# Scores of two chunks in one PSUM bank, fourteen transposes a pair, and the weight steps of DVE ahead of the divisions

## The chip, the cores and the metric

The kernel runs on one core of one Trainium2 chip. The metric is the device time of one execution in microseconds (us). Five engines work side by side, each through its own list of instructions in the order in which they were written: TensorE (PE, with its weight loads as PEld), VectorE (DVE), ScalarE (ACT), GpSimd (POOL) and SyncE (SP), which here only issues loads and stores. They wait for one another by semaphores.

## The reference

Attention, then a network with squared ReLU, then a gated network, all in float32:

```python
scores = scale * np.matmul(q, k.transpose(0, 1, 3, 2))      # 2 batches, 12 heads, 448 x 64
attn = np.exp(causal(scores) - max); attn = attn / (attn.sum(-1) + 1e-9)
x = np.matmul(attn, v)                                      # -> 896 tokens x 768
h = x @ w_in; x = (s * np.maximum(h, 0.0) ** 2 + b) @ w_out           # 768 -> 2048 -> 768
x = (1 / (1 + np.exp(-(x @ w_gate))) * (x @ w_val)) @ w_out2          # 768 -> 1536 -> 768
```

## The kernel before

The twelve pairs of heads are worked one after the other; the two heads of a pair lie side by side on the 128 partitions. The 448 queries of a head are cut into 7 chunks of 64, and chunk c needs the first (c + 1) x 64 keys, so that its scores are 64 to 448 columns wide. The two networks that follow are products of split numbers: an operand is held as a high and a low part, and three matmuls make one product.

For a pair, the work goes through these functions. `scores` (matmul at L242) writes the scores of one chunk into a PSUM bank of its own. `chunk` runs `softmax`: DVE adds the mask and takes the maximum (L229, two instructions, one of them the read of the maximum), ACT takes the exponential and the row sum (L232). `divide` (L261) has DVE make the reciprocals r of the sums (L265, L266) and POOL scale the seven chunks (L271). `turned` (L281) transposes the probabilities in blocks of 128 x 128 on PE (L291), four to a bank, four banks a pair; DVE copies the first and third bank (L279), ACT the second and fourth (L276). The fourth bank holds the blocks on the diagonal, of which only 64 rows are wanted. `values` (L313) multiplies with v into a bank of its own, `output_hi` (ACT, L276) and `output_lo` (DVE, L326) split the result into x_hi and x_lo.

The loop over i from 3 to 11 (L418 to L440) staggers this: pass i makes the scores of pair i, the values of pair i - 3, the softmax of pair i, the reciprocals and divisions of pair i - 1, and the transposes of pair i - 2. Its text is the order of each engine (`tc.manual_schedule()`): on PE a pass is scores, values, transposes; on DVE seven maxima with r behind the second, one step of the weights' splitting, copy, x_lo, copy; on ACT seven exponentials with x_hi behind the fifth, then two copies. The chunks go in the order

```python
ORDER = (0, 1, 6, 4, 3, 5, 2)
```

PSUM has eight banks: seven of tag "w", which scores and transposes take in turn, and one for the values. A bank is taken again only when its readers are through.

Into passes 4 to 10 the splitting of the first network's weights is woven, one step a pass (`split_steps`, L68; `step`, L354). A step of ACT (Abs at L75, the high part at L96) stands at the end of the pass, in passes 4, 8 and 10. A step of DVE stands behind the seventh maximum: L77 and L80 in pass 5, L85 in pass 6, L89 in pass 7, L98 in pass 9. L77 needs the Abs of pass 4, L98 the high part of pass 8.

Before the loop a prologue works pairs 0 to 2. The first pair's q and k come in four loads, two issued by SP and two by ACT; its chunks are made in the order 0 to 6. Behind the loop come the rest of the attention, between it the first matmuls of the first network (`fill`, L334), and the values of pair 11 end the attention.

Of the kernel before, what the change touches and what calls it, by code (L numbers as in the profile page):

```python
# [13 lines left out]
ALU = mybir.AluOpType  # L14
# [8 lines left out]
def body(ctx: ExitStack, tc: tile.TileContext, qk, vp, w_in, w_out, s, b, w_gate, w_val, w_out2, outT):  # L23
# [145 lines left out]
    with tc.tile_pool(name="at", bufs=2) as at:  # L169
# [5 lines left out]
        KF, KS = D, D + S + 4 * D  # L175
        Q_AT = {0: 0, 5: KF + S, 6: KF + S + D, 2: KS - 2 * D, 1: KS - D, 3: KS + 5 * D, 4: KS + 6 * D}
        ORDER = (0, 1, 6, 4, 3, 5, 2)

        PO, n = {}, 0
        for c in (0, 1, 2, 3, 4, 6, 5):  # L180
            PO[c], n = n, n + (c + 1) * D
        ALL = n

        mask = at.tile([P, S], F32, name="mask", bufs=1)
        nc.gpsimd.memset(mask, 0.0)
        for j in range(2):
            rows = slice(j * D, (j + 1) * D)
            nc.gpsimd.affine_select(
                out=mask[rows, S - D:], in_=mask[rows, S - D:], compare_op=ALU.is_ge, fill=NEG,
# [5 lines left out]
        HALF = slice(0, (NK - 1) * (NC + 2) + 1, NC + 2)  # L195
        for t in ptTs:
            nc.gpsimd.memset(t[D:, HALF], 0.0)
# [4 lines left out]
        def load_qk(i, engine=nc.sync):  # L202
# [31 lines left out]
        def scores(i, c):  # L234

            t = st[i]
            sc = t["sc", c] = bank("sc", "w")
            q0, n, k0 = Q_AT[c], (c + 1) * D, KF if c in FRONT else KS
            for j in range(2):
# [3 lines left out]
                    sc[j * D:(j + 1) * D, :n], t["qk"][rows, q0:q0 + D], t["qk"][rows, k0:k0 + n],  # L243
# [37 lines left out]
        def turned(i, copies=(dve, act, dve, act)):  # L281
# [21 lines left out]
            put(copies[3], t["ptT"][:D, HALF], [(2 * k, k) for k in range(NK)], D)  # L303
# [60 lines left out]
        with tc.manual_schedule():  # L364
# [53 lines left out]
            for i in range(3, N):  # L418
# [156 lines left out]
```

## Time and profile before

| | |
|---|---|
| median of three runs | 577.74 us (577.49 to 577.78) |
| the profiled execution | 577.84 us, its span 576.1 us |
| granted clock of TensorE in it | 1.00 |
| attention loop, passes 3 to 11 | 15.56 to 66.40 us of the span |
| end of the last attention product | 77.49 us |

The span is the time between the first and the last instruction that the profiler shows, the execution's own time has a little around it. Times in the timeline count from the start of the span. A matmul's end in it is modelled, and a line of the timeline may join several instructions of a line of the kernel (x28); the start of the next line then tells better how long the first took than its own duration. A line of the chain of waits says on which engine the work ran that the end of the kernel hung on.

### The profile page before, as it was taken

Reading aid. Unit: us, or ns where it says so; the run is one execution under the profiler, and the core shown is the slowest. Engines: PE = TensorE matmul, PEld = TensorE weight load, DVE = VectorE, ACT = ScalarE, POOL = GpSimd, SP = SyncE. Lnnn points to the kernel's source line nnn. Section 1 sums busy time; section 2 is a strip of 40 time slices with the busy share of each in tenths; the row PEclk is TensorE's granted clock in tenths of the full one; section 3 lists DMA queues with packets and bytes.
Section 4 is the critical chain, followed back from the end, with each engine's and each line's share of the span. In section 5 each row is a group of like instructions: output and inputs, shape, how many; then the busy total and the mean of one; then the engine's idle time right before and its main releaser. Section 6 shows DMA issues by size and latency. Waiting matters only on the chain.

```text
span 576.1 us, 8214 instructions
## 1 busy us (share of the span) xinstructions
PE 570.3 (99%) x3176; PEld 507.6 (88%) x3177; DVE 386.2 (67%) x705; ACT 266.8 (46%) x514; POOL 42.4 (7%) x93
## 2 busy tenths in 40 slices
PE   8999999999999999999999999999999999999997
PEld 4666789899999999999999999999999999999996
DVE  5899676999999766565647766666666666654000
ACT  6989846667776522223215333333333333332100
POOL 3676600000000000000000000000000000000000
PEclk9999999999999999999999999999999999999999
DMA  7745013345444333333322333333333333540000
GB/s 247 303 153 188 19 56 110 109 166 160 134 141 142 118 111 101 104 117 135 110 110 81 115 105 106 103 104 108 110 109 109 106 109 110 196 143 32 33 32 34
DMA packets 16168, 67.39 MB, mean 117 GB/s; under 512 B 2048, under 2 KB 3968, under 8 KB 16128
## 3 DMA queue, kind: packets, MB, share of 16 engines
q1 hardware_dynamic: 15696, 65.94, 34.7%
q10 hardware_dynamic: 432, 0.92, 0.5%
q8 instruction: 25, 0.41, 0.3%
q14 instruction: 15, 0.12, 0.1%
HBM read 64.10 MB, written 2.75 MB: 116 GB/s over the span
## 4 chain that ended last, share of the span: by engine, by line
PE 92%; ACT 4%; DVE 3%; issue 0%; DVEq 0%; ACTq 0%
PE acc L120 81%; PE po L313 4%; PE tp L291 3%; PE sc L242 3%; ACT pt L232 2%; DVE g L164 1%; DVE wt L85 0%; DVE wt L89 0%; ACT whi L96 0%; PE cold L373 0%; ACT ga_hi L165 0%; DVE wt L77 0%; DVE ga_lo L166 0%; DVE wlo L98 0%; ACT g L162 0%
## 5 line engine op out<-in xcount | busy, mean ns | idle before, releaser
L120 PE MATMUL acc<-x_hi,whi 128*128 128x448 f32 x480 | 175.6, 366 | 0.0
L120 PE MATMUL acc<-x_hi,wlo 128*128 128x448 f32 x480 | 175.4, 365 | 0.1
L120 PE MATMUL acc<-x_lo,whi 128*128 128x448 f32 x480 | 175.3, 365 | 0.0
L98 DVE TENSOR_TENSOR wlo<-wt,whi 128x768 fp32r<-128x768 f32 (+1 forms) x70 | 65.7, 939 | 74.5 <-ACT whi L96 74.3
L96 ACT ACTIVATE whi<-wt 128x768 fp32r<-128x768 f32 (+1 forms) x70 | 57.9, 827 | 122.2 <-PE acc L120 116.2
L120 PEld LDWEIGHTS acc<-x_hi,wlo 128*128 128x128 f32 x480 | 90.2, 188 | 7.6 <-DVE wlo L98 0.5
L120 PEld LDWEIGHTS acc<-x_hi,whi 128*128 128x128 f32 x480 | 90.2, 188 | 7.4 <-ACT whi L96 0.3
L120 PEld LDWEIGHTS acc<-x_lo,whi 128*128 128x128 f32 x480 | 90.2, 188 | 7.0
L75 ACT ACTIVATE wt<-raw 128x768 f32<-128x768 f32 (+1 forms) x70 | 61.7, 882 | 40.8 <-DVE wlo L98 31.2
L85 DVE SCALAR_TENSOR_TENSOR wt<-raw,wt 128x768 uint32<-128x768 uint32 (+1 forms) x70 | 65.9, 941 | 1.9
L89 DVE SCALAR_TENSOR_TENSOR wt<-raw,wt 128x768 uint32<-128x768 uint32 (+1 forms) x70 | 65.7, 938 | 1.1
L120 PE MATMUL acc<-gb_hi,whi 128*128 128x448 f32 x168 | 61.4, 365 | 0.0
L120 PE MATMUL acc<-gb_hi,wlo 128*128 128x448 f32 x168 | 61.4, 365 | 0.0
L120 PE MATMUL acc<-gb_lo,whi 128*128 128x448 f32 x168 | 61.4, 365 | 0.0
L77 DVE TENSOR_SCALAR wt<-wt 128x768 f32<-128x768 f32 (+1 forms) x70 | 38.7, 553 | 32.5 <-ACT wt L75 32.1
L120 PE MATMUL acc<-y_lo,whi 128*128 128x448 f32 x144 | 52.6, 365 | 0.0
L120 PE MATMUL acc<-y_hi,whi 128*128 128x448 f32 x144 | 52.6, 365 | 0.0
L120 PE MATMUL acc<-y_hi,wlo 128*128 128x448 f32 x144 | 52.6, 365 | 0.0
L232 ACT ACTIVATE pt<-pt,m 128x320 f32<-128x320 f32 (+6 forms) x84 | 41.7, 499 | 5.7 <-DVE m L229 5.6
L271 POOL TENSOR_SCALAR pt<-pt,r 128x128 f32<-128x128 f32 (+6 forms) x82 | 40.0, 511 | 27.8 <-DVE r L266 21.8
L507 ACT ACTIVATE y_hi<-y 128x448 fp32r<-128x448 f32 x24 | 13.9, 579 | 57.1 <-DVE y L506 57.1
L80 DVE TENSOR_SCALAR wt<-wt 128x768 uint32<-128x768 uint32 (+1 forms) x70 | 38.6, 552 | 2.0
(55 smaller groups left out, 599.6 us busy)
## 6 DMA issues: line engine op xcount, KB each, us to landing
raw<-in_w_out SPq DMA_DIRECT2D x18, 768.0 KB, 4.5
raw<-in_w_in SPq DMA_DIRECT2D x16, 768.0 KB, 4.3
raw<-in_w_gate SPq DMA_DIRECT2D x12, 768.0 KB, 4.3
raw<-in_w_val SPq DMA_DIRECT2D x12, 768.0 KB, 4.3
raw<-in_w_out SPq DMA_DIRECT2D x12, 640.0 KB, 4.1
qk<-in_qk SPq DMA_DIRECT2D x9, 608.0 KB, 4.6
vt<-in_vp SPq DMA_DIRECT2D x12, 256.0 KB, 4.6
outT<-ot SPq DMA_DIRECT2D x12, 224.0 KB, 1.9
```

What stands on the lines that cost most here:

```text
L75: nc.scalar.activation(out=f32(tt), in_=f32(high), func=AF.Abs)
L77: nc.vector.tensor_scalar(out=f32(tt), in0=f32(tt), scalar1=F64_TINY, scalar2=F64_HUGE, op0=ALU.max, op1=ALU.min,)
L80: nc.vector.tensor_scalar(out=tt, in0=tt, scalar1=0x07FFFFFF, scalar2=3, op0=ALU.bitwise_and, op1=ALU.logical_shift_left,)
L85: nc.vector.scalar_tensor_tensor(out=tt, in0=low, scalar=29, in1=tt, op0=ALU.logical_shift_right, op1=ALU.bitwise_or,)
L89: nc.vector.scalar_tensor_tensor(out=tt, in0=high, scalar=0xC0000000, in1=tt, op0=ALU.bitwise_and, op1=ALU.bitwise_or,)
L96: nc.scalar.activation(out=hif[:, :nn], in_=f32(tt), func=AF.Copy)
L98: nc.vector.tensor_tensor(out=lof[:, :nn], in0=f32(tt), in1=f32(hif[:, :nn]), op=ALU.subtract)
L120: nc.tensor.matmul(acc[:, :S], w[:, k - k0], m, start=k == 0 and i == 0, stop=k == K - 1 and i == 2)
L232: nc.scalar.activation(out=pc, in_=pc, func=AF.Exp, scale=-1.0, bias=m, accum_out=l)
L242: nc.tensor.matmul(sc[j * D:(j + 1) * D, :n], t["qk"][rows, q0:q0 + D], t["qk"][rows, k0:k0 + n], start=True, stop=True,)
L271: engine.tensor_scalar(out=probs(i, c), in0=probs(i, c), scalar1=st[i]["r"][:, c:c + 1], scalar2=1.0, op0=ALU.mult, op1=ALU.mult,)
L313: nc.tensor.matmul(po[j * D:(j + 1) * D, k * P:S].rearrange("p (c q) -> p c q", q=D), t["vt"][:, k, j], ptT[:, k, 2 * k:, j, :], start=k = ...
```

## The change

Three things change. First, chunks 0 and 5, 1 and 4, 3 and 2 put their scores into one bank, side by side (`SHARED`); chunk 6 keeps one alone. A pair then takes four banks for scores instead of seven. Second, the probabilities are laid out so that the fourth bank needs two transposes instead of four: the seven blocks on the diagonal are written as fourteen halves by ACT, one copy for each half of the partitions (two instructions of 64 partitions x 256 instead of one of 64 x 512). For that, keys, mask and v are laid out in another order, the mask is 832 columns wide instead of 448, and POOL zeroes four pieces instead of two at the start. The loads have the same bytes; the first pair's four parts are 160 and 160 KB on SP, 192 and 96 KB on ACT, before 64 and 256 KB, 160 and 128 KB, and the second pair's two parts 320 and 288 KB instead of 256 and 352. Third, a DVE step of the weights stands behind the second maximum and ahead of r, so ahead of POOL's divisions, and x_lo stands behind both of DVE's copies. The steps of ACT stay where they are.

```diff
-        KF, KS = D, D + S + 4 * D
-        Q_AT = {0: 0, 5: KF + S, 6: KF + S + D, 2: KS - 2 * D, 1: KS - D, 3: KS + 5 * D, 4: KS + 6 * D}
+
+        Q_AT = {c: n * D for c, n in ((5, 0), (6, 1), (0, 9), (4, 10), (3, 11), (1, 17), (2, 18))}
+        K_AT = {c: n * D for c, n in ((0, 5), (5, 3), (6, 2), (1, 14), (2, 13), (3, 12), (4, 12))}
         ORDER = (0, 1, 6, 4, 3, 5, 2)
+        SHARED = {0: 5, 5: 0, 1: 4, 4: 1, 2: 3, 3: 2}
 
         PO, n = {}, 0
-        for c in (0, 1, 2, 3, 4, 6, 5):
+        for c in (0, 2, 4, 6, 1, 3, 5):
             PO[c], n = n, n + (c + 1) * D
         ALL = n
...
+        BLOCK = {
+            (c, k): PO[c] + n * D for (c, k), n in {
+                (1, 0): 0, (2, 0): 1, (3, 0): 2, (4, 0): 2, (5, 0): 2, (6, 0): 3,
+                (3, 1): 0, (4, 1): 0, (5, 1): 0, (6, 1): 1, (5, 2): 4, (6, 2): 5,
+            }.items()
+        }
...
-        HALF = slice(0, (NK - 1) * (NC + 2) + 1, NC + 2)
+
+        HALVES = [(slice(j * D, (j + 1) * D), slice(j * (NC + 2), (j + 2) * (NC + 2) + 1, 2 * (NC + 2))) for j in range(2)]
         for t in ptTs:
-            nc.gpsimd.memset(t[D:, HALF], 0.0)
+            for j in range(2):
+                nc.gpsimd.memset(t[HALVES[1 - j][0], HALVES[j][1]], 0.0)
...
-                    (nc.sync, 0, KF + D), (nc.scalar, Q_AT[2], KS + 3 * D),
-                    (nc.sync, KF + D, Q_AT[2]), (nc.scalar, KS + 3 * D, W),
+                    (nc.sync, K_AT[0], Q_AT[4]), (nc.scalar, K_AT[2], W),
+                    (nc.sync, 0, K_AT[0]), (nc.scalar, Q_AT[4], K_AT[2]),
                 ):
                     eng.dma_start(out=t[:, a:b], in_=qk[bb, hp, :, a:b])
             elif i == 1:
-                for a, b in ((0, KS - 4 * D), (KS - 4 * D, W)):
+                for a, b in ((0, Q_AT[4]), (Q_AT[4], W)):
...
-            sc = t["sc", c] = bank("sc", "w")
-            q0, n, k0 = Q_AT[c], (c + 1) * D, KF if c in FRONT else KS
+            if c in SHARED and ("sc", SHARED[c]) in t:
+                sc = t["sc", SHARED[c]]
+                a = S - (c + 1) * D
+            else:
+                sc, a = bank("sc", "w"), 0
+            t["sc", c] = sc
+            t["at", c] = a
+            q0, n, k0 = Q_AT[c], (c + 1) * D, K_AT[c]
             for j in range(2):
                 h = j if c in FRONT else 1 - j
                 rows = slice(h * D, (h + 1) * D)
                 nc.tensor.matmul(
-                    sc[j * D:(j + 1) * D, :n], t["qk"][rows, q0:q0 + D], t["qk"][rows, k0:k0 + n],
+                    sc[j * D:(j + 1) * D, a:a + n], t["qk"][rows, q0:q0 + D], t["qk"][rows, k0:k0 + n],
                     start=True, stop=True,
...
-            softmax(probs(i, c), t["sc", c][:, :n], mask[:, S - n:], t["m"][:, c:c + 1], t["l"][:, c:c + 1])
+            m0 = M0 if c in (2, 3, 6) else S - n
+            softmax(probs(i, c), t["sc", c][:, t["at", c]:t["at", c] + n], mask[:, m0:m0 + n], t["m"][:, c:c + 1], t["l"][:, c:c + 1])
...
-            def put(copy, out, blocks, rows=P):
+            def put(copy, out, blocks):
                 tp = bank("tp", "w")
-                for n, (c, k) in enumerate(blocks):
-                    a = PO[c] + k * P
-                    nc.tensor.transpose(tp[:, n * P:(n + 1) * P], t["pt"][:, a:a + P], ident)
-                tp = tp[:rows].rearrange("p (n q) -> p n q", q=P)
+                for n, b in enumerate(blocks):
+                    nc.tensor.transpose(tp[:, n * P:(n + 1) * P], t["pt"][:, BLOCK[b]:BLOCK[b] + P], ident)
...
-            put(copies[3], t["ptT"][:D, HALF], [(2 * k, k) for k in range(NK)], D)
+            tp = bank("tp", "w")
+            for n, a in enumerate((PO[0], PO[6] - D)):
+                nc.tensor.transpose(tp[:, n * P:(n + 1) * P], t["pt"][:, a:a + P], ident)
+            for rows, at_blocks in HALVES:
+                copies[3](t["ptT"][rows, at_blocks], tp[rows, :2 * P].rearrange("p (n q) -> p n q", q=P))
...
+                late = following[0] == "act"
                 for n, c in enumerate(ORDER):
                     chunk(i, c)
                     if n == 1:
+                        if 4 <= i < N - 1 and not late:
+                            step()
                         divide(i - 1)
                     if n == 4:
                         output_hi(i - 3)
-                late = following[0] == "act"
-                if 4 <= i < N - 1 and not late:
-                    step()
-                t = turned(i - 2)
-                next(t)
+                for _ in turned(i - 2):
+                    pass
                 output_lo(i - 3)
-                for _ in t:
-                    pass
                 if 4 <= i < N - 1 and late:
```


DVE in pass 6, from its first maximum to the end of its pass; before (sc are scores, m the maxima, tp transposes, ptT their copy, wt and raw the weights; a wait names the engine or load waited for; the reads of the maxima between are left out):

```order
L229 ISA pt,m<-sc,mask 128x64 [waits PE_49,Pool_49]
L229 ISA pt,m<-sc,mask 128x128 [waits PE_49]
L265 TENSOR_SCALAR r<-l 128x7 [waits Activation_49]
L266 RECIPROCAL r<-r 128x7 [waits DVE_49]
L229 ISA pt,m<-sc,mask 128x448 [waits PE_49]
...
L229 ISA pt,m<-sc,mask 128x192 [waits PE_49]
L85 SCALAR_TENSOR_TENSOR wt<-raw,wt 128x768 [waits DMAHW5_49]
L279 COPY ptT_97<-tp 128x512 [waits PE_49]
L326 TENSOR_TENSOR x_lo<-po,x_hi 128x448 [waits Activation_49]
L279 COPY ptT_97<-tp 128x2x256 [waits PE_49]
```


and now:

```order
L241 ISA pt,m<-sc,mask 128x64 [waits PE_49,Pool_49]
L241 ISA pt,m<-sc,mask 128x128
L85 SCALAR_TENSOR_TENSOR wt<-raw,wt 128x768 [waits DMAHW5_49]
L284 TENSOR_SCALAR r<-l 128x7 [waits Activation_49]
L285 RECIPROCAL r<-r 128x7 [waits DVE_49]
L241 ISA pt,m<-sc,mask 128x448
L241 ISA pt,m<-sc,mask 128x320
...
L298 COPY ptT_97<-tp 128x512 [waits PE_49]
L298 COPY ptT_97<-tp 128x2x256 [waits PE_49]
L348 TENSOR_TENSOR x_lo<-po,x_hi 128x448 [waits Activation_49]
```


The step moved from behind the seventh maximum to behind the second, r went behind it, x_lo behind the second copy. The first maximum now waits for the matmul of chunk 5, the last writer of its bank, and the following ones, that of chunk 3 aside, for nothing of their own.

PE in pass 6, its scores and the first values (the first of two matmuls of a chunk carries the wait); before:

```order
L242 MATMUL sc<-qk 64x64 [waits DMAHW0_49,DVE_49]
L242 MATMUL sc<-qk 64x128 [waits DVE_49]
L242 MATMUL sc<-qk 64x448 [waits DVE_49]
L242 MATMUL sc<-qk 64x320 [waits DVE_49]
L242 MATMUL sc<-qk 64x256 [waits Activation_49]
L242 MATMUL sc<-qk 64x384 [waits DVE_49]
L242 MATMUL sc<-qk 64x192 [waits Activation_49]
L313 MATMUL po<-ptT_98,vt 64x448 [waits DMAHW1_49]
L313 MATMUL po<-ptT_98,vt 64x320 x2
```


and now:

```order
L260 MATMUL sc<-qk 64x64 [waits DMAHW0_49,DVE_49,PE_49]
L260 MATMUL sc<-qk 64x128 [waits DVE_49,PE_49]
L260 MATMUL sc<-qk 64x448 [waits DVE_49,PE_49]
L260 MATMUL sc<-qk 64x320 x2
L260 MATMUL sc<-qk 64x256 [waits DVE_49]
L260 MATMUL sc<-qk 64x384 x2
L260 MATMUL sc<-qk 64x192 x2
L335 MATMUL po<-ptT_98,vt 64x448 [waits DMAHW1_49,DVE_49,Activation_49]
L335 MATMUL po<-ptT_98,vt 64x320 [waits Activation_49]
```


The scores have four waits for a bank's readers instead of seven (PE's waits for itself are for matmuls of the pass before). The first product of values, which had only waited for its load, now waits for DVE and for ACT's first half copy, the next for ACT's second.

PE in the first pair; before:

```order
L242 MATMUL sc<-qk 64x64 [waits DMAHW1_49]
L242 MATMUL sc<-qk 64x128 [waits DMAHW0_49]
L242 MATMUL sc<-qk 64x192 x2
L242 MATMUL sc<-qk 64x256 [waits DMAHW2_49]
L242 MATMUL sc<-qk 64x320 x2
```


and now:

```order
L260 MATMUL sc<-qk 64x64 [waits DMAHW1_49]
L260 MATMUL sc<-qk 64x128 [waits DMAHW0_49]
L260 MATMUL sc<-qk 64x192 x2
L260 MATMUL sc<-qk 64x256 [waits DMAHW3_49,DVE_49]
L260 MATMUL sc<-qk 64x320 x2
```


The scores of chunk 3 (256 wide) now also wait for DVE, the maximum of chunk 2 in the same bank.

## Rows read from the trace of the kernel before

**Rows 1.** The page, part 1: busy time, share of the span, instructions of each engine.
```profile
PE 570.3 (99%) x3176; PEld 507.6 (88%) x3177; DVE 386.2 (67%) x705; ACT 266.8 (46%) x514; POOL 42.4 (7%) x93
```

**Rows 2.** Windows over passes 3 to 11; columns in the row above the numbers.
```profile
core 0: us, PE busy (x) PEld busy (x) DVE busy (x) ACT busy (x) POOL busy (x), PEclk, DMA share, GB/s
15.56:66.40 50.84, 50.81 (x541) 34.41 (x541) 46.23 (x180) 47.88 (x162) 33.77 (x68) 1.00 0.53 186
```

**Rows 3.** Windows, same stretch, the score matmuls (L242) alone: stretch, span, PE, PEld.
```profile
15.56:66.40 50.84, 17.55 (x252) 9.24 (x252) 1.00 0.53 186
```

**Rows 4.** Timeline of PE: start us, us, engine, line, operation, tiles, count.
```profile
38.57 2.04 PE L242 MATMUL sc<-qk 64*64 64x64 f32 x28
...
50.06 1.74 PE L242 MATMUL sc<-qk 64*64 64x64 f32 x28
51.74 1.95 PE L313 MATMUL po<-ptT,vt 128*64 128x448 f32 x16
53.62 1.97 PE L291 MATMUL tp<-ident,pt 128*128 128x128 f32 x16
55.51 1.82 PE L242 MATMUL sc<-qk 64*64 64x64 f32 x28
...
68.25 3.68 PE L313 MATMUL po<-ptT,vt 128*64 128x448 f32 x32
...
77.49 0.47 PE L120 MATMUL acc<-x_hi,whi 128*128 128x448 f32 x1
```

**Rows 5.** Chain of waits in order of time: start us, us, engine, tile, line, instructions.
```profile
10.34 4.21 ACT pt L232 x16
...
18.59 1.80 ACT pt L232 x6
...
78.15 0.73 ACT whi L96
78.88 0.81 ACT wt L75
...
106.01 4.12 PE acc L120 x19
```

**Rows 6.** Timeline of DVE, pass 7 and the start of pass 8.
```profile
39.61 0.21 DVE L229 CUSTOM_DVE_ANT_0 pt<-sc,mask 128x64 f32<-128x64 f32 x1
...
40.28 0.57 DVE L229 CUSTOM_DVE_ANT_0 pt<-sc,mask 128x448 f32<-128x448 f32 x1
...
42.29 1.42 DVE L89 SCALAR_TENSOR_TENSOR wt<-raw,wt 128x768 uint32<-128x768 uint32 x1
43.63 0.68 DVE L279 COPY ptT<-tp 128x512 f32<-128x512 f32 x1
...
45.36 0.21 DVE L229 CUSTOM_DVE_ANT_0 pt<-sc,mask 128x64 f32<-128x64 f32 x1
```

**Rows 7.** Timeline of POOL: the seven divisions of pass 7.
```profile
40.55 3.91 POOL L271 TENSOR_SCALAR pt<-pt,r 128x128 f32<-128x128 f32 x7 [1.85 <-DVE r L266]
```

**Rows 8.** Timeline of DVE, weight steps behind the attention loop, POOL idle.
```profile
74.29 0.55 DVE L77 TENSOR_SCALAR wt<-wt 128x768 f32<-128x768 f32 x1
...
75.47 0.96 DVE L85 SCALAR_TENSOR_TENSOR wt<-raw,wt 128x768 uint32<-128x768 uint32 x1
...
91.36 0.96 DVE L85 SCALAR_TENSOR_TENSOR wt<-raw,wt 128x768 uint32<-128x768 uint32 x1
92.23 0.51 DVE L164 TENSOR_SCALAR g<-g,s_sb,b_sb 128x448 f32<-128x448 f32 x1
```

**Rows 9.** Timeline of ACT, pass 7; in brackets idle time before and its releaser.
```profile
39.87 0.35 ACT L232 ACTIVATE pt<-pt,m 128x64 f32<-128x64 f32 x1 [0.49 <-DVE m L229]
...
40.89 0.67 ACT L232 ACTIVATE pt<-pt,m 128x448 f32<-128x448 f32 x1 [0.20 <-DVE m L229]
...
44.06 1.06 ACT L276 ACTIVATE ptT<-tp 128x512 f32<-128x512 f32 x2
```

**Rows 10.** Timeline of the first pair: weight loads of PE and a maximum of DVE.
```profile
4.69 0.32 PEld L242 LDWEIGHTS sc<-qk 64*64 64x64 f32 x8 [0.53 <-DMA qk<-in_qk]
4.82 0.36 DVE L229 CUSTOM_DVE_ANT_0 pt<-sc,mask 128x192 f32<-128x192 f32 x1 [0.30 <-PE sc L242]
```

More of the change, by code (lines that the diff above doesn't have):

```diff
@@ L173, in body @@
         FRONT, SWAP = (0, 5, 6), (2, 1, 3, 4)
-        KF, KS = D, D + S + 4 * D
-        Q_AT = {0: 0, 5: KF + S, 6: KF + S + D, 2: KS - 2 * D, 1: KS - D, 3: KS + 5 * D, 4: KS + 6 * D}
+        Q_AT = {c: n * D for c, n in ((5, 0), (6, 1), (0, 9), (4, 10), (3, 11), (1, 17), (2, 18))}
+        K_AT = {c: n * D for c, n in ((0, 5), (5, 3), (6, 2), (1, 14), (2, 13), (3, 12), (4, 12))}
         ORDER = (0, 1, 6, 4, 3, 5, 2)
+        SHARED = {0: 5, 5: 0, 1: 4, 4: 1, 2: 3, 3: 2}
         PO, n = {}, 0
-        for c in (0, 1, 2, 3, 4, 6, 5):
+        for c in (0, 2, 4, 6, 1, 3, 5):
             PO[c], n = n, n + (c + 1) * D
         ALL = n
-        mask = at.tile([P, S], F32, name="mask", bufs=1)
+        BLOCK = {
[4 more added lines that the diff above has]
+        }
+        M0 = S - D
+        mask = at.tile([P, M0 + S], F32, name="mask", bufs=1)
         nc.gpsimd.memset(mask, 0.0)
@@ L188, in body @@
             nc.gpsimd.affine_select(
-                out=mask[rows, S - D:], in_=mask[rows, S - D:], compare_op=ALU.is_ge, fill=NEG,
+                out=mask[rows, M0:S], in_=mask[rows, M0:S], compare_op=ALU.is_ge, fill=NEG,
                 base=0, channel_multiplier=1, pattern=[[-1, D]],
@@ L285, in turned @@
             by_k = t["ptT"].rearrange("p (k c) q -> p k c q", c=NC)
-            def put(copy, out, blocks, rows=P):
+            def put(copy, out, blocks):
                 tp = bank("tp", "w")
-                for n, (c, k) in enumerate(blocks):
-                    a = PO[c] + k * P
-                    nc.tensor.transpose(tp[:, n * P:(n + 1) * P], t["pt"][:, a:a + P], ident)
-                tp = tp[:rows].rearrange("p (n q) -> p n q", q=P)
+                for n, b in enumerate(blocks):
+                    nc.tensor.transpose(tp[:, n * P:(n + 1) * P], t["pt"][:, BLOCK[b]:BLOCK[b] + P], ident)
+                tp = tp.rearrange("p (n q) -> p n q", q=P)
                 if len(out.shape) == 4:
@@ L543, in part @@
         return [x[..., c * 64:c * 64 + 64] for c in chunks]
-    qS, kS = qT[:, :, ::-1], kT[:, :, ::-1, :, :5 * 64]
+    qS, kS = qT[:, :, ::-1], kT[:, :, ::-1]
     qk = np.concatenate(
-        [*part(qT, 0), kT, *part(qT, 5, 6), *part(qS, 2, 1), kS, *part(qS, 3, 4)], axis=-1,
+        part(qT, 5, 6) + part(kT, 6, 3, 2, 0, 1, 4, 5) + part(qT, 0)
+        + part(qS, 4, 3) + part(kS, 3, 2, 0, 1, 4) + part(qS, 1, 2), axis=-1,
     )
     vp = np.zeros((B, NP, 128, 4, 2, D), v.dtype)
-    for j in range(2):
-        for c in range(4):
-            w = min(128, S - c * 128)
-            vp[:, :, :w, c, j] = v[:, j::2, c * 128:c * 128 + w]
+    for a, (c, r) in enumerate(((0, 0), (0, 64), (1, 64), (1, 0), (2, 0), (2, 64), (3, 64))):
+        for j in range(2):
+            vp[:, :, r:r + 64, c, j] = v[:, j::2, a * 64:a * 64 + 64]
     arrays = {
```

## Prediction

> **What bounds the kernel now.** Start with the busy line of the page [rows 1]: PE works 99% of the span, so a microsecond counts only if it is PE work taken away or PE waiting added or taken away. The change touches attention alone, so next comes the table of windows over passes 3 to 11 of the attention loop [rows 2]: in 50.84 us PE is busy 50.81, ACT 47.88, DVE 46.23. PE leads, but ACT is only 3 us behind it over nine passes, which is thin cover. The same window for the score matmuls alone [rows 3] shows 17.55 us for nine stretches. PE's timeline [rows 4] tells what a stretch needs: in pass 9 scores run 1.68 us from their start to that of values (50.06 to 51.74), values 1.88, the sixteen transposes 1.89; the slow stretch of pass 7 was recorded at 2.04 against 1.74. So 17.55 - 9 x 1.74 = 1.9 us of the score stretches is waiting inside them, for banks. Then the chain of waits [rows 5]: in the prologue it runs on ACT's exponentials (10.34 to 14.55, again at 18.59), through the passes on PE, after the last product on the weight splits of ACT and DVE (78.15, 78.88), and from 106.01 on PE again. PE never rests there [rows 1], so a delay of the last attention product, whose end is at 77.49 [rows 4], passes whole to the end of the kernel. The sum is therefore made for that moment.
>
> **What is taken away.** Two transposes of sixteen a pass: 1.89 / 16 = 0.118 us each, so 1.89 becomes 1.66; twelve pairs give 2.8 us. With four score banks instead of seven, a score stretch no longer waits inside for the copies of the transposes but for one bank: up to 1.9 us. If nothing else came in, that would be 4.7 us.
>
> **What is added on the path.** First DVE's opening. In pass 7 the maximum of chunk 0 began at 39.61 [rows 6], 1.04 after the scores' start at 38.57 [rows 4]. Now the order shows that it waits for the matmul of chunk 5, the sixth of seven, since both lie in one bank; by the modelled ends that is the recorded stretch of 1.74, and I add 0.03 for the signal: 1.77. DVE itself would be free earlier, by an estimate at U + 1.11: the third group of transposes ends 0.24 before the scores' start U, and a signal of 0.22, a copy of 0.6 and x_lo of 0.53 follow (the copy and x_lo as they stood between 43.63 and 45.36 [rows 6]). With C0 at U + 1.11 the whole sum below would be -0.2, with U + 1.77 it is +1.15.
>
> The Trainium skill ("PSUM — Partial Sum Buffer", section "PSUM bank collisions raise a hardware error") says that DVE may not read a bank while PE writes other columns of the same partitions in it, and that one guards by bank and not by address. That rule speaks against this change: by it the wait costs the difference of those two sums, and a finer one is not to be had. No row here shows such a collision.
>
> Then the weight step. It moves ahead of r and of chunk 6's maximum. Beside POOL's divisions L89 took 1.42 [rows 6] while POOL worked from 40.55 to 44.46 [rows 7]; without POOL L85 starts 0.87 before its follower, and L77 with L80 take 75.47 - 74.29 = 1.18 [rows 8]. In the new place POOL is idle, so I charge 0.87 in passes 6 and 7, 0.88 in 9 and 1.18 in 5. DVE saves time by it; but before, the step stood behind the seventh maximum, with exponentials, x_hi and copies still before ACT. Now ACT has the exponentials of chunks 0 and 1, which cover an estimated 0.74 us (39.87 to 40.89, waits taken off [rows 9]).
>
> The Trainium skill ("SBUF — State Buffer", section "SBUF: two separate sides") calls the port that DVE and GpSimd share an exclusive lock whose loser blocks wholly, and the 1.42 of L89 against the 0.96 of L85 without POOL agrees. By it alone the move is gain, 0.46 us of DVE a step; the sum would have that only if DVE's work, and not its order, were what PE waits for.
>
> **The cycle, with its prices.** For each pass U is the start of its scores, V that of its values, C0 and C6 the starts of the maxima of chunks 0 and 6, E6 that of chunk 6's exponential, F when ACT is through.
> - C0 = U + 1.77, or the DVE's own end of the pass before, C6 + 3.74: from 40.28 to 45.36 it was 5.08 [rows 6], less 1.34 for the step (42.29 to 43.63).
> - C6 = C0 + 0.67 (39.61 to 40.28 [rows 6]) + the step. In passes 5 and 9 the step also waits for ACT's piece at the end of the pass before, + 0.15 for the signal, and 0.32 for r follows it.
> - E6 = C6 + 0.61 (40.28 to 40.89 [rows 6, 9]), or F + 0.74.
> - F = E6 + 4.21: before, 4.23 from 40.89 to the recorded end of the two copies, 44.06 + 1.06 [rows 9], of which 0.08 lie beside the next instruction; the fourth copy in two halves adds an estimated 0.06, bounded with the release below. Abs adds 0.81 in passes 4 and 10, L96 adds 0.73 in pass 8 [rows 5].
> - next V = next U + 1.68, or E6 + 4.08: the order shows values waiting for ACT's first half copy, 0.27 before F, and I add 0.14 for the signal, both estimates. Bounds: 3.80 if it is released by the bare half, 4.30 if by both halves with their signal.
> - next U = V + 1.88 + 1.66.
>
> A pass without a step thus repeats every (1.77 + 1.28 + 4.08 + 3.54) / 2 = 5.33 us, since E6 of one pass releases V of the next: better than the 50.84 / 9 = 5.65 of before, worse than PE's own 5.22. A step lengthens this loop by nearly its full length.
>
> **Prologue.** The first load is 160 KB instead of 64, and chunk 3's scores wait for chunk 2's maximum, which shares its bank. Before, they could start with their load at 4.69; that maximum ran from 4.82 to 5.18 [rows 10]. ACT works without rest from 10.34 on [rows 5], so a delay there is handed on. Bounds: 0 (ACT's chain catches it) and 0.75 (those 0.49 and half as much again for the larger first load); I take 0.35, near the middle. POOL's longer set-up, the ACT instructions more and the moved loads, of the same bytes, stand beside this and are in the 0.75.
>
> **The sum.** U of pass 3 was 15.56 [rows 2] and becomes 15.91, E6 18.96 (was 18.59 [rows 5]). By the rules V of passes 4 to 11 is 23.04, 28.26, 35.54, 40.82, 47.08, 52.30, 58.93, 64.15; pass 9 was 51.74 [rows 4]. Three of these are set by ACT after a step: pass 6 after L77 and L80 (E6 31.46), pass 8 after L89 (43.00), pass 10 after L98 (54.85). The values of pair 9 come at 65.56 + 4.08 = 69.64, before at 68.25; from there to the end it was 9.24, now 9.00 with two transposes less: 78.64 against 77.49, **1.15 us later**. x_lo behind both copies is in C6 + 3.74 and costs nothing while U + 1.77 is later; only pass 6 starts on DVE's end (34.59 against 33.57). Chunk 1's bank in the next pass now waits for chunk 5's maximum, C6 + 1.8, late by 0.8 in pass 5 alone, where DVE is late anyway. The profiled execution took 577.84 (its span 576.1), 0.10 above the median 577.74; so 577.84 + 1.15 = **579.0**.
>
> What the terms are worth: prologue 0 or 0.75 gives +0.80 or +1.55; release 3.80 or 4.30 gives +0.6 or +1.8; steps hidden wholly -1.5; steps half as long again +2.6.
>
> **Rivals.** One, *faster*: ACT trails DVE far enough that the step is covered. Place: the gap before the 448-wide exponential in passes 5, 6, 7, 9. It decides if ACT is busy until 1.4 us after C0 there. Against: in pass 7 ACT started 0.26 after C0 and already waited before 40.89 [rows 6, 9]. For: ACT loses no work, and after Abs it does trail. It gives -1.5, 576.3; ACT's own 47.88 + 9 x 0.06 of 50.84 [rows 2] forbid more than -2.4, so 575.4 is the floor. Chance 0.23.
>
> Two, *no change*: the prologue absorbs its delay and values are released by the bare half: +0.24, 578.1, and with half of each step hidden too -0.7, 577.2. The losses and the 2.8 us of transposes then cancel. For: every signal is charged above. Against: the same arithmetic makes the nine passes of the old order some 0.5 us too short. Chance 0.20.
>
> Three, *slower still*: the step meets POOL after all, because POOL's 3.9 us of divisions [rows 7] begin later in step passes, and takes 1.42: +2.6, 580.5. It needs divisions that last beyond the next C0; they have over 0.4 us to spare. Chance 0.12.
>
> That the change doesn't do what it says is excluded for the transposes by the order; that scores wait inside the stretch as before is part of the range.
>
> **How the numbers follow.** 0.2% of 577.74 is 1.16 us, about what a measurement of this kernel can tell from no change. The forecast keeps 0.45, its own range 577.9 to 580.4 by the terms above; its middle lies at that border, and as the arithmetic erred on the short side I give 0.31 of it to slower and 0.14 to the same. With rival two the same is 0.34, with rival three slower is 0.43, faster is 0.23. The range runs from the floor of rival one, 575.4, to 581.0 (prologue at 0.75 and steps at 1.42 are +3.0, 580.9).
>
> **What would show it.** Right: DVE waits for PE before its 64-wide maximum, 1.7 to 1.8 after the scores' start; score stretches at 1.74; L85, L89, L98 at 0.96; ACT idle for DVE before the 448-wide exponential, by about a microsecond in passes 5, 6, 7, 9; PE idle before values for ACT's copy in passes 6, 8, 10; attention's last product ending near 78.6. Wrong: PE gapless at 5.22 to 5.33 a pass through the step passes (rival one), or steps still at 1.42 (rival three). A first exponential of pass 1 no later than before takes 0.35 off.

## The result

Over seven executions each, the changed kernel takes 582.72 us (median) where the kernel before takes 577.78; the ratio is 1.0073 with a 95% interval of [1.0063, 1.0084], so 4.2 us slower. Profiled and timed again beside another series of the kernel before (e9 below) it is 1.0069 [1.0055, 1.0083]. The direction was forecast; 579.0 was not, and the time lies above the range's upper end of 581.0, though two of the five executions behind it, 580.63 and 580.66 us, lie inside the range. Some executions of every kernel, the one before included, take about 1.6% longer (586.4 to 587.2 us for the kernel before), with the networks' matmuls slower (486 instead of 495 in the 100 us from 200 on), and they are left out of the ratios. The rows below come from e9, the same kernel again, in an execution of 581.66 us (span 579.9). Attention's own times are the same in the changed kernel's first profile (63.47 us from pass 3 to the last product there, 63.51 in e9, and as close in the pairs e5 and e10, e8 and e11 below), so that these can be compared over all profiles.

### The profile page after: what moved, and what is told of

Read it like the earlier page. It is cut to its first block, busy times and chain, and to the rows that moved or that the text cites. A ratio compares the mean times of both kernels' runs of the same rounds, so it can differ in the third digit from the quotient of the medians.

```text
span 588.5 us, 8206 instructions
## 1 busy us (share of the span) xinstructions
PE 576.5 (98%) x3152; PEld 504.9 (86%) x3153; DVE 385.6 (66%) x705; ACT 271.2 (46%) x526; POOL 40.4 (7%) x95
## 4 chain that ended last, share of the span: by engine, by line
PE 85%; ACT 8%; DVE 5%; issue 1%; DMA 1%; ACTq 0%; DVEq 0%
PE acc L120 81%; ACT pt L244 5%; PE po L335 2%; ACT ptT L295 1%; DVE pt L241 1%; PE sc L260 1%; PE tp L309 1%; DVE wt L89 1%; DVE g L164 1%; ACT whi L96 1%; DMA qk<-in_qk 1%; DVE wt L85 0%; DVE wlo L98 0%; DVE wt L77 0%; ACT wt L75 0%
## 5 line engine op out<-in xcount | busy, mean ns | idle before, releaser
L85 DVE SCALAR_TENSOR_TENSOR wt<-raw,wt 128x768 uint32<-128x768 uint32 (+1 forms) x70 | 65.4, 934 | 1.9
L89 DVE SCALAR_TENSOR_TENSOR wt<-raw,wt 128x768 uint32<-128x768 uint32 (+1 forms) x70 | 65.2, 931 | 1.1
L77 DVE TENSOR_SCALAR wt<-wt 128x768 f32<-128x768 f32 (+1 forms) x70 | 38.3, 547 | 33.5 <-ACT wt L75 33.1
L80 DVE TENSOR_SCALAR wt<-wt 128x768 uint32<-128x768 uint32 (+1 forms) x70 | 38.4, 548 | 2.0
L290 POOL TENSOR_SCALAR pt<-pt,r 128x128 f32<-128x128 f32 (+6 forms) x82 | 37.4, 480 | 33.6 <-DVE r L285 29.5
```

What stands on the lines that cost most here:

```text
L77: nc.vector.tensor_scalar(out=f32(tt), in0=f32(tt), scalar1=F64_TINY, scalar2=F64_HUGE, op0=ALU.max, op1=ALU.min,)
L80: nc.vector.tensor_scalar(out=tt, in0=tt, scalar1=0x07FFFFFF, scalar2=3, op0=ALU.bitwise_and, op1=ALU.logical_shift_left,)
L85: nc.vector.scalar_tensor_tensor(out=tt, in0=low, scalar=29, in1=tt, op0=ALU.logical_shift_right, op1=ALU.bitwise_or,)
L89: nc.vector.scalar_tensor_tensor(out=tt, in0=high, scalar=0xC0000000, in1=tt, op0=ALU.bitwise_and, op1=ALU.bitwise_or,)
L290: engine.tensor_scalar(out=probs(i, c), in0=probs(i, c), scalar1=st[i]["r"][:, c:c + 1], scalar2=1.0, op0=ALU.mult, op1=ALU.mult,)
```

## The profile after

PE's timeline of the changed kernel, score stretches and values of passes 3 to 11 and of the last pairs; columns as in [rows 4], in brackets the idle time before and its releaser:

```profile
15.90 1.75 PE L260 MATMUL sc<-qk 64*64 64x64 f32 x28
17.57 1.95 PE L335 MATMUL po<-ptT,vt 128*64 128x448 f32 x16
...
32.83 0.33 PE L260 MATMUL sc<-qk 64*64 64x64 f32 x4
33.70 1.89 PE L260 MATMUL sc<-qk 64*64 64x128 f32 x24 [0.54 <-DVE m L241]
36.55 1.95 PE L335 MATMUL po<-ptT,vt 128*64 128x448 f32 x16 [0.96 <-ACT ptT L295]
...
40.10 1.74 PE L260 MATMUL sc<-qk 64*64 64x64 f32 x28
42.10 1.95 PE L335 MATMUL po<-ptT,vt 128*64 128x448 f32 x16 [0.25 <-ACT ptT L295]
...
48.36 1.95 PE L335 MATMUL po<-ptT,vt 128*64 128x448 f32 x16 [0.96 <-ACT ptT L295]
...
53.65 1.95 PE L335 MATMUL po<-ptT,vt 128*64 128x448 f32 x16
...
60.91 1.95 PE L335 MATMUL po<-ptT,vt 128*64 128x448 f32 x16 [0.96 <-ACT ptT L295]
...
72.31 3.68 PE L335 MATMUL po<-ptT,vt 128*64 128x448 f32 x32 [0.94 <-ACT ptT L295]
...
79.41 1.95 PE L335 MATMUL po<-ptT,vt 128*64 128x448 f32 x16
```

Pass 3 starts at 15.90 where it was 15.56 [rows 2], the last attention product at 79.41 where it was 75.61, in the kernel before:

```profile
75.61 1.95 PE L313 MATMUL po<-ptT,vt 128*64 128x448 f32 x16
```

So 0.34 us came in ahead of the loop, and from there to the last product it takes 63.51 us instead of 60.05: 3.46 more. The execution is 581.66 - 577.84 = 3.82 longer, and 0.34 + 3.46 = 3.80: the whole loss is made before the last product of attention and passes one to one to the end.

The waits of PE and of ACT (us in total, times, longest; PE's up to the last product, ACT's in the loop) say where; the last line is the kernel before:

```profile
PE po L335 <- ACT ptT L295: 4.9, 6, 1.0
PE sc L260 <- DVE m L241: 1.0, 2, 0.5
```

```profile
ACT pt L244 <- DVE m L241: 3.7, 5, 1.3
```

```profile
ACT pt L232 <- DVE m L229: 2.8, 9, 0.6
```

Of PE's gaps, 4.9 us stand ahead of values, for ACT's copies of the transposes, and 1.0 ahead of chunk 1's scores; before, PE had none to speak of [rows 2]. ACT in turn waits 3.7 us for DVE, where it was 2.8. The windows over the nine passes, all engines and then the score matmuls alone:

```profile
15.90:69.44 53.54, 48.48 (x521) 32.90 (x521) 44.66 (x179) 49.20 (x166) 30.31 (x67) 1.00 0.50 175
```

```profile
15.90:69.44 53.54, 16.65 (x252) 9.94 (x252) 1.00 0.50 175
```

PE's work fell from 50.81 to 48.48 and its score stretches from 17.55 [rows 3] to 16.65, as meant; but ACT's rose from 47.88 to 49.20, and PE, which had waited for nothing, now waits for ACT's copies. **The bound has moved from PE to ACT.** (ACT's busy time and its waiting together, 52.9 of 53.54, would not show it: before they were 50.7 of 50.84. PE's waiting does, and e6 and e14 below.) ACT's timeline of pass 5, up to the first exponential of pass 6, shows the two parts of its pass, the wait for DVE and the longer work behind it:

```profile
32.35 0.67 ACT L244 ACTIVATE pt<-pt,m 128x448 f32<-128x448 f32 x1 [1.32 <-DVE m L241]
...
33.56 0.49 ACT L244 ACTIVATE pt<-pt,m 128x256 f32<-128x256 f32 x1
33.96 0.19 ACT L244 ACTIVATION_READ_ACCUMULATOR pt<-pt,m 128x1 f32 x1
34.17 0.54 ACT L295 ACTIVATE x_hi<-po 128x448 fp32r<-128x448 f32 x1
...
35.65 1.25 ACT L295 ACTIVATE ptT<-tp 128x512 f32<-128x512 f32 x3
36.52 0.38 ACT L295 ACTIVATE ptT<-tp 64x256 f32<-64x256 f32 x1
36.92 0.35 ACT L244 ACTIVATE pt<-pt,m 128x64 f32<-128x64 f32 x1
```

The row at 36.52 is the last of the three copies by itself. The 448-wide exponential waits 1.32 for DVE, which is at L77 and L80. Then it is 36.92 - 32.35 = 4.57 us to the first exponential of the next pass. Before it was 4.13, as in pass 8, where the next instruction also follows at once (50.77 - 46.64):

```profile
46.64 0.67 ACT L232 ACTIVATE pt<-pt,m 128x448 f32<-128x448 f32 x1 [0.20 <-DVE m L229]
...
49.81 1.06 ACT L276 ACTIVATE ptT<-tp 128x512 f32<-128x512 f32 x2
50.77 0.83 ACT L96 ACTIVATE whi<-wt 128x768 fp32r<-128x768 f32 x1
```

The values of pass 6 start at 36.55, 4.20 after the 448-wide exponential. The copies by shape, first before (passes 3 to 11), then now:

```profile
L276 ACT ACTIVATE ptT<-tp 64x512 f32<-64x512 f32 x9 | 5.2, 583 | 0.0
```

```profile
L295 ACT ACTIVATE ptT<-tp 64x256 f32<-64x256 f32 x18 | 6.7, 373 | 0.2
...
L295 ACT ACTIVATE ptT<-tp 128x512 f32<-128x512 f32 x8 | 4.7, 582 | 0.0
```

A copy of half the size takes 373 ns and not half of 583, but that is the smaller part. Before, the instruction behind the fourth copy started 0.10 us ahead of that copy's end (49.81 + 1.06 = 50.87, and 50.77); now it starts 0.02 behind the end of the second half copy (36.52 + 0.38 = 36.90, and 36.92), and the second half copy starts 0.02 behind the end of the first. So the three copies take 36.92 - 35.65 = 1.27 us where two took 50.77 - 49.81 = 0.96, 0.31 less; the remaining 0.13 of the 0.44 is x_hi's, which has lost its overlap too, as told at the end.

DVE and POOL, pass 7, with the step L89 in its new place:

```profile
41.99 0.23 DVE L241 CUSTOM_DVE_ANT_0 pt<-sc,mask 128x64 f32<-128x64 f32 x1 [0.78 <-PE sc L260]
...
42.35 0.95 DVE L89 SCALAR_TENSOR_TENSOR wt<-raw,wt 128x768 uint32<-128x768 uint32 x1
```

```profile
43.81 3.21 POOL L290 TENSOR_SCALAR pt<-pt,r 128x128 f32<-128x128 f32 x7 [3.06 <-DVE r L285]
```

The first maximum waits 0.78 for PE and comes at 41.99, 1.89 after the scores' start at 40.10. L89 takes 0.95 and not 1.42 [rows 6], POOL's seven divisions 3.21 and not 3.91 [rows 7]: that part of the forecast held.

## The experiments

Three questions: which of the three edits loses how much, whether ACT's pass is the term that was mis-sized, and why the changed kernel's times fall into groups (580.6 to 580.8, 581.6 to 581.8, 582.4 to 582.8) where those of the kernel before lie within 577.0 and 578.6 but for one. Each kernel's attention is compared by its profile: the start of pass 3, the start of the last product, and the time between, which leaves the prologue out. Where too few executions are left for a ratio, their times stand in its place.

| kernel | ratio to before, 95% interval | pass 3 | last product | between |
|---|---|---|---|---|
| before | | 15.56 | 75.61 | 60.05 |
| e9, changed again | 1.0069 [1.0055, 1.0083] | 15.90 | 79.41 | 63.51 |
| e1, sharing alone | 1.0042 [1.0026, 1.0057] | 17.11 | 78.48 | 61.37 |
| e2, fourteen transposes alone | 1.0004 [0.9994, 1.0014] | 15.23 | 75.90 | 60.67 |
| e3, new order of the loop alone | 1.0023 [1.0014, 1.0033] | 15.83 | 77.39 | 61.56 |
| e4, changed, old order of the loop | 1.0031 [1.0020, 1.0043] | 16.98 | 78.21 | 61.23 |
| e5 and e10, changed, first pair unshared | e5: one, 580.75; e10: 1.0060 [1.0046, 1.0075] | 15.70, 15.38 | 79.17, 78.89 | 63.47, 63.51 |
| e6, changed, a half copy on DVE | 1.0028 [1.0009, 1.0047], of two | 14.80 | 75.49 | 60.69 |
| e7, changed, partners adjacent | none (589.4 to 591.5) | 17.17 | 79.96 | 62.79 |
| e8 and e11, four edits | e8: none (584.5 to 585.3); e11: 0.9967 [0.9954, 0.9980] | 15.02, 15.60 | 73.39, 73.94 | 58.37, 58.34 |
| e12, e11 with x_lo between | 1.0031 [1.0019, 1.0042] | 14.99 | 76.98 | 61.99 |
| e13, changed, x_lo in its old place | 1.0075 [1.0051, 1.0099], of two | 15.80 | 79.30 | 63.50 |
| e14, changed, steps last | 1.0006 [0.9995, 1.0017] | 17.37 | 77.31 | 59.94 |
| e15, before, steps last | one, 577.13 | 15.38 | 75.31 | 59.93 |

### The three parts one by one (e1 to e4)

**e1** puts the sharing alone on the kernel before:

```diff
-            sc = t["sc", c] = bank("sc", "w")
+            if c in SHARED and ("sc", SHARED[c]) in t:
+                sc = t["sc", SHARED[c]]
+                a = S - (c + 1) * D
+            else:
+                sc, a = bank("sc", "w"), 0
...
```

> Only the sharing of banks, on the kernel before: sixteen transposes, one ACT copy of the fourth bank, steps behind the seventh maximum. Theory A (the loss is made along one loop, first maximum to ACT's last copy to values, and every part of the change that lengthens it costs): the first maximum 0.85 us later after the scores' start than before gives +0.9 to +1.5 us, 578.6 to 579.3. Theory B (the whole loss is the steps' new place; sharing only frees the score stretches): -1.0 to -1.9 us, about 576.3. In the profile: first maximum 1.9 us after the scores' start by both.

**e2** has a bank for every chunk and the loop of before:

```diff
-        SHARED = {0: 5, 5: 0, 1: 4, 4: 1, 2: 3, 3: 2}
+        SHARED = {}
```

> The changed kernel with a bank for every chunk again and the loop in its old order: fourteen transposes and ACT's half copies alone. Theory A: 2.8 us of PE work taken away and ACT's pass 0.37 longer nearly cancel, 577.4 to 578.4. Theory B: the transposes count in full, 575.0 to 575.8. The half copies take 0.77 us a pass where one copy took 0.49.

**e3** puts the changed loop (step behind the second maximum, x_lo behind both copies) on the kernel before, and **e4** puts the loop of before into the changed kernel; both are the last piece of the diff above, once forward and once backward.

> Only the loop's new order (steps behind the second maximum, x_lo behind both copies) on the kernel before. Theory A: without the longer loop of the other two parts the steps cost +0.4 to +1.4 us, 578.1 to 579.1. Theory B: +3 us or more, 580.7 and over.

> The changed kernel with the loop in its old order: sharing and fourteen transposes together. Theory A: +0.8 to +1.7 us, 578.5 to 579.4. Theory B: -1 us or below, under 576.8. Theory C (ACT's half copies alone make the loss, wherever the steps stand): +2.5 us or more, 580.2 and over.

Measured against 60.05 us from pass 3 to the last product: sharing +1.32, fourteen transposes +0.62, the new order +1.51, the first two together +1.18, all three +3.46. No single part makes the loss, so theories B and C fall, and every part costs by itself in the attention, as theory A had it. Two sizes were off. Sharing cost 2.4 us in its time (2.9 in the profiled execution) where 0.9 to 1.5 was expected; 1.5 of it stands in the prologue (pass 3 at 17.11), which is the third question. And the new order costs more on the other two parts (63.51 - 61.23 = 2.28) than alone, which fits ACT's longer pass: nothing takes up the delay.

### ACT's pass and the first maximum (e6, e7)

**e6** gives DVE one half copy, ahead of ACT's:

```diff
-            for rows, at_blocks in HALVES:
-                copies[3](t["ptT"][rows, at_blocks], tp[rows, :2 * P].rearrange("p (n q) -> p n q", q=P))
+            for copy, (rows, at_blocks) in zip((copies[2], copies[3]), HALVES):
+                copy(t["ptT"][rows, at_blocks], tp[rows, :2 * P].rearrange("p (n q) -> p n q", q=P))
```

> The changed kernel, but DVE makes one of the two half copies of the fourth bank, ahead of ACT's. Theory A (ACT's pass, 0.37 us longer from chunk 6's exponential to its end, is the mis-sized term): my rules with 4.21 for that pass give 2.0 to 2.6 us less than the changed kernel, 578.1 to 578.7, and up to 2 more where the prologue is long. Theory D (DVE's order is what binds, so more work on DVE costs as much as ACT gains): no change, 580.2 to 582.7.

From pass 3 to the last product it is 60.69, 2.8 us less than the changed kernel, a little more than the rules' 2.0 to 2.6; theory D falls. (One of its eleven executions took 1498 us, which nothing here explains.) What is late next shows in PE's timeline of e6, passes 7 and 8: values now wait 0.30 for DVE's x_lo.

```profile
39.81 1.95 PE L335 MATMUL po<-ptT,vt 128*64 128x448 f32 x16 [0.30 <-DVE x_lo L348]
...
45.41 1.95 PE L335 MATMUL po<-ptT,vt 128*64 128x448 f32 x16 [0.30 <-DVE x_lo L348]
```

**e7** has PE make the two chunks of a bank one after the other, from pass 3 on:

```diff
-                for c in ORDER:
+                for c in (0, 5, 1, 4, 6, 3, 2):
                     scores(i, c)
```

> The changed kernel, but from pass 3 on PE makes the scores of two chunks that share a bank one after the other (0, 5, 1, 4, 6, 3, 2), DVE and ACT in their old order. Theory A (the first maximum's wait for chunk 5 is a link of the loop): the first maximum comes 1.1 to 1.3 us after the scores' start instead of 1.89, and the time falls by 0.7 to 0.8 us, to 579.8 or 581.9 by the prologue. Theory E (only the steps' place and ACT's pass bind): the first maximum comes earlier and the time stays within 0.2 us of the changed kernel's.

62.79 instead of 63.51, 0.7 less: the first maximum, in pass 7 now 1.14 after the scores' start and not 1.89, is a link, as theory A says, and worth what was expected. This rests on the profile alone.

### Which edit of the new order (e13, e14, e15)

The new order holds two edits. **e13** puts x_lo back between DVE's copies; **e14** leaves x_lo and moves the steps to the end of DVE's pass; **e15** does the same to the kernel before.

```diff
                     if n == 1:
-                        if 4 <= i < N - 1 and not late:
-                            step()
                         divide(i - 1)
...
                 output_lo(i - 3)
-                if 4 <= i < N - 1 and late:
+                if 4 <= i < N - 1:
                     step()
```

> The changed kernel with x_lo between DVE's copies again, the steps still behind the second maximum. Theory A (the early step starves ACT; x_lo's place does nothing): within 0.4 us of the changed kernel, 580.5 to 582.8, PE waiting for ACT's copy before the values of passes 6, 8 and 10 as before this edit. Theory X (the new place of x_lo, which holds the next first maximum, makes the loop's share of the loss): 1 us or more faster, under 579.8.

> The changed kernel with DVE's steps at the end of its pass, behind x_lo, nothing else changed. Theory A: the steps leave the way from the first maximum to ACT's last copy, and the rules give 3.3 us less of the loop: 577.3 to 578.2 with an early clock, up to 1.5 more with a late one. Theory X: x_lo's place stays, so no more than 1.5 us are won, 579.2 and over.

> The kernel before with DVE's steps at the end of its pass, behind both copies, in place of behind the seventh maximum. Theory A: copies and x_lo come 1.3 us earlier in four passes, values are released earlier, at most 0.3 us is won: 577.2 to 577.8. Rival: the step now holds the next first maximum, slower, 578.3 or more.

x_lo's place does nothing (63.50 against 63.51). The steps' place does everything: 59.94, 3.6 us less, where the rules gave 3.3. PE's timeline of e14, the scores and values of pass 7, then ACT's of pass 5 (first row) and of pass 6, whose copies these values read:

```profile
40.11 1.74 PE L260 MATMUL sc<-qk 64*64 64x64 f32 x28
41.84 1.95 PE L335 MATMUL po<-ptT,vt 128*64 128x448 f32 x16
```

```profile
32.36 0.67 ACT L244 ACTIVATE pt<-pt,m 128x448 f32<-128x448 f32 x1
...
36.92 0.35 ACT L244 ACTIVATE pt<-pt,m 128x64 f32<-128x64 f32 x1
...
37.27 0.39 ACT L244 ACTIVATE pt<-pt,m 128x128 f32<-128x128 f32 x1
...
37.66 0.66 ACT L244 ACTIVATE pt<-pt,m 128x448 f32<-128x448 f32 x1
```

No wait for DVE stands ahead of the 448-wide exponential in pass 5, where it was 1.32, and in pass 6, where it was 0.15; in pass 7 it is 0.20 instead of 0.85, in pass 9 none instead of 1.12. Over the loop ACT waits 0.5 us for DVE, where it was 3.7, and PE up to the last product 3.6 for ACT's copies, where it was 4.9. The end of the pass is also free of POOL, whose divisions of pass 6 are through at 40.51, so the steps take 0.95 there too and not the 1.43 that L85 takes in e4, behind the seventh maximum:

```profile
41.13 0.95 DVE L85 SCALAR_TENSOR_TENSOR wt<-raw,wt 128x768 uint32<-128x768 uint32 x1
```

These runs do not part the two gains of that place. That the fourteen transposes save PE 2.8 us and the kernel nothing is seen here as well: 59.94 is 0.1 under the kernel before. On the kernel before, where ACT has 4.13 and not 4.57 a pass, the steps' last place is worth as little (59.93).

### The prologue (e5, e9, e10)

**e5**, and again **e10** beside **e9**, give the first pair a bank for every chunk:

```diff
-            if c in SHARED and ("sc", SHARED[c]) in t:
+            if i and c in SHARED and ("sc", SHARED[c]) in t:
```

> The changed kernel, but the first pair's seven chunks have a bank each, so that its scores wait for no maximum of the same pair. Theory P (the wait of chunk 3's scores in the first pair lets PE pause while its clock is still low, and in a part of the executions the clock then rises later and the prologue is some 1.5 us longer, as in the run with the old loop, whose pass 3 begins at 16.98): the executions near 582.6 vanish and the rest stays, 580.2 to 580.9, and pass 3 begins at 15.2 to 15.6. Theory Q (the prologue has no part in it): both groups of times stay, median 581 to 582.7.

> The changed kernel again, for the spread of its times beside the next run. Theory P (the pause of PE in the first pair, and a clock that rises before or long after it): times in two groups, near 580.6 and near 582.6. Theory Q: the earlier groups were chance, one group around 581.5.

> The changed kernel with a bank for every chunk of the first pair, in the same batch as the changed kernel. Theory P: one group, 580.2 to 581.0, none near 582.6. Theory Q: the same spread as the changed kernel's.

For e10 one group was expected, and none of its times is near 582.6: the times of e5 and e10 that are kept for ratios are 580.58 to 581.17, those of the changed kernel 580.63 to 582.79. For e9 two groups were expected, and that was a miss: it has one time of 580.75 and three of 581.6 to 581.8, none near 582.6, and the middle group is not explained. Over all profiles, pass 3 starts between 14.99 and 15.83 in the nine whose first pair is not shared; where it is shared it is 14.80 to 15.90 in four of eight (the changed kernel's first profile among them, 15.39) and 16.98 to 17.37 in the other four. The first pair's larger load has no part in that: e2 has it and starts pass 3 at 15.23. What the four have in common, in PE's timeline of e14 (first row) and of e9 (second), and then in the 448-wide score matmuls between 7.6 and 9 us, of e14 and of e9:

```profile
5.79 6.17 PE L260 MATMUL sc<-qk 64*64 64x256 f32 x56 [0.47 <-DVE m L241]
```

```profile
5.57 3.90 PE L260 MATMUL sc<-qk 64*64 64x256 f32 x44 [0.47 <-DVE m L241]
```

```profile
L260 PE MATMUL sc<-qk 64*64 64x448 f32 x6 | 2.7, 951 | 0.0
```

```profile
L260 PE MATMUL sc<-qk 64*64 64x448 f32 x6 | 1.4, 537 | 0.0
```

Both pause 0.47 us for the maximum of chunk 2. In e9 the same matmul then takes 537 ns, in e14 951: by these durations TensorE is still at the lower of its two levels there, 1.2 GHz. The traces' record of the granted clock agrees: the full level, 2.4 GHz, is first on it at 7.14 us of the span in e9 and at 10.20 in e14. (Ahead of that the record is empty, and the windows show 1.00 for want of it.) Over all profiles the full level is first on record at 9.67 to 10.20 in the four late ones, and at 4.24 to 7.64 in the thirteen others, 6.96 in the kernel before, which has no pause ahead of it. In two of the eight that share, the level had risen before the pause (4.24 and 5.18); of the six that paused while it was low, two rose at 7.0 and 7.1 and four late. So the wait that sharing brings into the first pair does not itself cost 1.5 us; it leaves PE a gap while its clock is low, and in a part of the executions the clock then rises some 3 us later. That the gap brings the late rise is argued from its absence in all profiles without it; why it goes one way or the other in an execution of one and the same kernel is open.

### A version that beats both (e8, e11, e12)

**e8**, and again **e11**, have the edits of e5, e6, e7 and e14 together; **e12** has x_lo between the copies besides.

> All three together, and DVE's weight steps at the end of its pass, behind both copies, the half copy and x_lo. Theory A: the rules give the last attention product 1.3 to 2.1 us earlier than before; they were up to 0.9 short for other orders, so 575.6 to 577.3. A rival: the steps at the end delay the next first maximum, which starts the next loop, and PE waits again: 577.7 or more.

> First pair unshared, one half copy on DVE, partners adjacent on PE, DVE's weight steps at the end of its pass, once more, for times to set against the kernel before. In the profile of the run before, its last attention product began at 73.39 where the kernel before has 75.61; if that passes whole to the end, 575.2 to 575.8. Rival: part of it is given back behind the attention, 576.5 or more.

> The same, with x_lo between DVE's two copies again. In the profile PE waited 0.29 us for x_lo in two passes; x_lo comes 0.95 earlier, the second copy and DVE's half 0.53 later, still ahead of ACT's half. Theory A: 0.3 to 0.6 us less, 574.8 to 575.5. Rival: the copies become what values wait for, no change or slower.

e11 is 1.9 us faster than the kernel before (0.9967, interval [0.9954, 0.9980]), 575.51 against 577.40, as was expected of it, and its last product starts at 73.94, 1.7 earlier. The windows of e11 over its nine passes:

```profile
15.60:64.54 48.94, 47.84 (x523) 32.61 (x523) 46.92 (x189) 46.78 (x157) 30.91 (x68) 1.00 0.54 194
```

PE has 47.84 of 48.94 us, ACT 46.78, DVE 46.92: PE bounds again. e12 was a miss: 0.3 to 0.6 us was to be won, 3.7 was lost. DVE's timeline shows that x_lo waits there for ACT's x_hi, and with it the second copy and the half copy, which values now wait for (PE's row):

```profile
37.27 0.69 DVE L298 COPY ptT<-tp 128x512 f32<-128x512 f32 x1
38.28 0.62 DVE L348 TENSOR_TENSOR x_lo<-po,x_hi 128x448 fp32r<-128x448 f32 x1 [0.32 <-ACT x_hi L295]
38.82 1.00 DVE L298 COPY ptT<-tp 128x512 f32<-128x512 f32 x2
```

```profile
39.88 1.95 PE L335 MATMUL po<-ptT,vt 128*64 128x448 f32 x16 [0.89 <-DVE ptT L298]
```

I had counted x_lo's end and not the wait ahead of it, which is 0.3 us in six of the nine passes and 1.0 to 1.1 in the other three, on the way of everything behind.

## Why the prediction was wrong

**What held.** PE was the bound, and the end of attention passes one to one to the end (3.80 and 3.82). The stretches of scores came to 1.74 but for two that wait 0.5, the transposes to 1.67. The wait of the first maximum for the whole score stretch, the steps at 0.95 and POOL at 3.2 are there as described, and so is the starving of ACT in passes 5, 7 and 9 (1.32, 0.85, 1.12); in pass 6 it is only 0.15. The starts of values that the rules gave, 23.04, 28.26, 35.54, 40.82, 47.08, 52.30, 58.93, 64.15 and 69.64, are 23.71, 29.00, 36.55, 42.10, 48.36, 53.65, 60.91, 66.20 and 72.31: the same three passes, 6, 8 and 10, open latest, each 0.96 after PE was ready. Against the rules the values fall behind in passes 4, 6, 7 and 10 and again at the last, not in pass 8.

**The step that failed** is the rule F = E6 + 4.21, with "the fourth copy in two halves adds an estimated 0.06". Measured, F = E6 + 4.57: two half copies cost 0.31 more than the one copy, not 0.06, and x_hi another 0.12 (below). About 0.06 is what two copies of 373 ns would cost beyond one of 583 if each overlapped the next instruction by 0.10 as before; the step took for granted that ACT's instructions go on overlapping, and three of them a pass no longer do. Put into the rules, 4.57 alone raises the sum from 1.15 to 3.04. The release at 4.20 and not 4.08, and the first maximum at 1.89 and not 1.77, bring it to 3.52, against 3.80 measured at nearly the prologue that was assumed (0.34 for 0.35); the last 0.3 are not accounted for. e6, which takes one half copy off ACT, gives 2.8 us back. The range missed it for a reason of its own: the half copies' cost was "bounded with the release below", 3.80 to 4.30, but it enters in a second place, where the next pass's exponentials start (F + 0.74). With 4.57 + 0.74 = 5.31 ACT's own round is as long as the loop's 5.33, so no pass can win back what a step has cost. Before it was 4.13 + 0.74 = 4.87, against PE's 5.65.

**Rivals.** Rival one needed ACT to be busy until 1.4 us after the first maximum's start; its first exponential came 1.19 after it in pass 6 (36.92 - 35.73) and 0.49 in pass 7 (42.48 - 41.99), so the steps were not covered, and the rival's floor from 47.88 + 9 x 0.06 was wrong by the same term, since ACT has 49.20. Rival two needed the release by the bare half, 3.80, and no delay in the prologue; it was 4.20, and 0.34. Rival three came nearest in size, for a wrong reason: no step meets POOL. The prologue's 0.35 was right in this execution by luck; by the clock it lies between -0.8 and 0.3 in four profiles and between 1.4 and 1.8 in the four others.

**The two rules of the Trainium skill.** That of "PSUM — Partial Sum Buffer", section "PSUM bank collisions raise a hardware error", decided as expected: the program keeps to it, so the first maximum waits for the partner's matmul, and e7 shows what an order that respects it more cheaply gets back, 0.7 of the 1.35 that lay between the two sums. What the chip would do without that wait no run here shows. That of "SBUF — State Buffer", section "SBUF: two separate sides", agrees too (0.95 without POOL, 1.42 beside it), and as said it was no gain while the order starved ACT.

## What to carry to other kernels

Before work is taken off the engine that bounds, work out the round of the next one with every instruction that the change gives it; the split of one small copy in two cost 0.31 us where 0.06 was set, since instructions that had overlapped no longer did, and such a cost counts twice where the engine's end releases one thing and starts another. An engine that feeds the next bound should do its long pieces when the fed engine has work in hand: the same weight steps cost 3.6 us more behind the second maximum than at the end of the pass, and in both places they run without POOL. And judge a change in parts: fourteen transposes, shared banks and uncontended steps each do what they should, and the version with all of them in other places is 1.9 us faster than before.

## What was not expected of the hardware

- A copy of 64 x 256 from PSUM on ACT takes 373 ns, one of 64 x 512 583: half the columns are not half the time.
- A pause of 0.47 us while TensorE was at its lower level: of six profiles that have it, the full level is first on record at 7.0 and 7.1 us in two and at 9.67 to 10.20 in four, and in these four pass 3 starts some 1.5 us later; without such a pause it is 4.24 to 7.64 in all eleven.
- Three of ACT's starts lose their overlap in all kernels with the fourteen transposes. The second half copy starts 0.02 us behind the end of the copy ahead of it, the instruction behind it 0.02 behind its end, and x_hi 0.02 behind the end of the sum's read (in e9's pass 5 it starts 0.61 after the exponential, at 34.17). In the kernel before, e1, e3 and e15, whose fourth copy is in one piece, that copy, the instruction behind it and x_hi start about 0.10 ahead of such an end, x_hi 0.49 after the exponential, wherever ACT does not wait for another engine. Each loss is 0.12 us in every pass of ACT, together 0.37, about what F = E6 + 4.21 was short. It goes with the new layout of the probabilities; what in it does this was not tried.
